# Two tokens per row for k and v, an attention output with fewer and wider matmuls, and a convolution by full diagonals, in a fused linear-attention and gated-unit kernel

## The chip, the cores and the metric

The kernel runs on one core of one Trainium2 chip. The metric is the device time of one execution in microseconds (us). Each kernel was run several times; medians are quoted with the number of runs. The medians are over all executions. Some of these were slow, which here means over 1.5% above the fastest of the same kernel in its job. The ratios use fast executions alone, and every profiled execution was a fast one. A profile's span is some 2 us shorter than the time of the same run (127.0 against 128.8 us for the kernel before).

Names of engines in the profile: PE is the matrix engine (PEld its weight loads), DVE the vector engine, ACT the scalar engine, POOL the general one, SP the one that issues the DMA transfers. PSUM is the memory that PE writes its results to. "Full clock" is a granted PE clock of 1.0 in the profile's records; before the first such record the matmuls ran at about half the pace. A "hole" is a stretch in which PE stands still without a wait that the profile shows.

## The reference

Four sequences of 768 tokens, eight heads of 48 channels. A recurrence keeps a 48x48 state per head; its output goes, heads side by side (384 channels), into a gated unit with a causal convolution of five taps.

```python
for t in range(S):
    cur = np.einsum('bhd,bhe->bhde', u[None] * kt, vt)          # bonus for the token itself
    y[:, :, t] = np.einsum('bhd,bhde->bhe', rt, state + cur)
    state = w[None, :, :, None] * state + np.einsum('bhd,bhe->bhde', kt, vt)
# x = y with the heads side by side
gate = sigmoid(sum over 5 taps of conv_w[tap] * shifted x)
val = x @ w_val
out = (gate * val) @ w_out
```

## The kernel before

Tokens are handled in chunks of 128. One pass of the main loop takes a unit of two chunks (cl = 0, 1) through one of four stages each: k transposes for unit i; bonus, scores, mask and state for unit i-1; attention output for unit i-2; convolution, value and projection for unit i-3. There are 12 units, so the loop has 15 passes.

```python
def load_kv(n, which):                       # 192 bytes per row and head
    ...
    d[n] = ld.tile([128, U, H, D], F32, name=f"{nm}_st")
    for cl in range(U):
        t0 = cu * W + cl * C
        nc.sync.dma_start(out=d[n][:, cl], in_=src[b, :, t0 : t0 + C, :].transpose([1, 0, 2]))

def y_out(n):                                # attention output: 32-column tiles
    for cl in range(U):
        y_ps = ps_mm.tile([128, NT, 128], F32, name="mm_ps")
        ...                                  # mm(G, ...): 32 columns, column group q = G % 4
        for G in range(3 * NP):              # state part
            mm(G, zf[:, 32 * G : 32 * G + 32], rT[:, G // 3, cl * C : cl * C + C])
        for x in range(2):                   # score part
            for h in range(H):
                ...
                mm(3 * p + (1 if x else 2 * par), vb[:, cl, 64*h+c0 : 64*h+c0+32], at[:, par, p, :])
        for G in range(3 * NP):              # bonus part
            mm(G, dv[:, cl, 32 * G : 32 * G + 32], ident, last=True)
        nc.scalar.copy(out=xT_t[b % 2][:, :, t0 : t0 + C], in_=y_ps)

def conv(n):                                 # 32x32 diagonals on 32x32 tiles
    for T0 in (0, 2):
        for t in range(KW):
            for q in range(4):
                for i in range(2):
                    ...
                    nc.tensor.matmul(out=g_ps[i][32*qo : 32*qo+32, o0 : o0+n0],
                                     lhsT=cwdiag[rows, T, t, :], rhs=xT[rows, T, ...], ...)
```

"Column group" below means one of the four strips of 32 columns of the PE array, set by the partitions that a matmul writes to; "row half" one of its two halves of 64 rows, set by the partitions that it reads. A "tile" of the array is a row part with a column part.

## Time and profile before

| | before |
|---|---|
| time, median of 4 runs | 128.5 us (128.04 to 129.91) |
| span of the profiled execution | 127.0 us |
| first convolution matmul | 34.2 us |
| PE matmuls | 2667 |
| chain that ended last | PE 58%, SPq 18%, issue 7%, DVE 6% |

The kernel has a first stage in which the loads fill the DMA engines, and a second stage from the first convolution on in which PE carries the chain. The chain is followed back from the last instruction, at each step to what released it. These are the three longest of the six waits of PE in the second stage of the kernel before (window 34 to 122 us): who waited for whom, then us in total, times, longest.

```profile
PE mm_ps L420 <- issue: 5.4, 3, 2.6
PE mm_ps L420 <- DVE cwdiag L206: 2.3, 1, 2.3
PE mm_ps L283 <- issue: 1.1, 2, 0.8
```

L420 is the convolution. "issue" means that PE stood still and the profile shows nothing that it waited for.

### The profile page before, as it was taken

What the parts mean: (1) busy time and instruction counts of PE and PEld (TensorE: products, weight loads), DVE (VectorE), ACT (ScalarE), POOL (GpSimd) and SP (SyncE); (2) the same over time, 40 slices, a digit from 0 to 9 for tenths busy, and PEclk for the clock granted to TensorE, in tenths of its full rate; (3) what the DMA queues carried; (4) which work ended last, traced back from release to release, by engine and by line L of the source; (5) the groups of instructions that cost most, each with busy time, mean ns of one, the idle gap of its engine ahead of it and who ended that gap; (6) DMA issues with size and microseconds to landing.
All of it is one profiled execution on the core that took longest, in us unless ns stands there. A gap on an engine that the chain in (4) does not pass through costs nothing.

```text
span 127.0 us, 5936 instructions
## 1 busy us (share of the span) xinstructions
PE 96.4 (76%) x2667; PEld 73.7 (58%) x2667; DVE 80.7 (64%) x134; ACT 64.6 (51%) x113; POOL 63.0 (50%) x90
## 2 busy tenths in 40 slices
PE   0036864865299749979994899999999999999950
PEld 0024643453188537767872666778777777777620
DVE  0559578733929619859695296596968978663030
ACT  4599800235452823745946506559492656264630
POOL 6925561485929807059796250597967050500000
PEclk9999999999999999999999859999999999999999
DMA  1999999999997979787599983973030030303203
GB/s 47 189 341 222 194 242 300 204 337 197 198 201 158 334 149 273 155 211 154 158 299 228 245 164 69 241 141 129 0 129 5 0 126 8 132 5 124 105 24 124
DMA packets 58675, 20.83 MB, mean 164 GB/s; under 512 B 50453, under 2 KB 58650, under 8 KB 58650
## 3 DMA queue, kind: packets, MB, share of 16 engines
q1 hardware_dynamic: 58522, 20.46, 66.0%
q8 instruction: 20, 0.33, 1.1%
q0 software_dynamic: 128, 0.00, 0.1%
q14 instruction: 5, 0.04, 0.1%
HBM read 15.74 MB, written 4.72 MB: 161 GB/s over the span
## 4 chain that ended last, share of the span: by engine, by line
PE 58%; SPq 18%; issue 7%; DVE 6%; DMA 4%; ACT 2%; DVEq 0%
PE mm_ps L420 11%; PE mm_ps L376 11%; SPq L72 10%; PE mm_ps L468 9%; PE mm_ps L439 6%; SPq L80 6%; PE at_ps L310 5%; DMA k_st<-in_k_dram 4%; PE tr_ps L263 4%; PE kv_ps L336 3%; PE mm_ps L448 3%; PE tr_ps L238 2%; PE mm_ps L283 2%; PE kv_ps L345 2%; ACT o_sb L475 2%
## 5 line engine op out<-in xcount | busy, mean ns | idle before, releaser
L296 POOL TENSOR_TENSOR dv<-v_st,s_sb 128x384 bf16<-128x384 f32 x24 | 19.4, 829 | 33.7 <-PE at_ps L310 31.5
L322 DVE TENSOR_TENSOR at<-at_ps,mask 128x1024 bf16<-128x1024 f32 x24 | 29.3, 1220 | 2.5 <-PE at_ps L310 1.6
L404 ACT CAST xT<-mm_ps 128x384 bf16<-128x384 f32 x24 | 11.5, 478 | 30.0 <-PE mm_ps L376 29.4
L255 POOL CAST vb<-v_st 128x384 bf16<-128x384 f32 x24 | 17.1, 733 | 9.1 <-DMA v_st<-in_v_dram 9.1
L420 PE MATMUL mm_ps<-xT,cwdiag 32*32 32x256 bf16 (+1 forms) x960 | 15.5, 253 | 7.7 <-issue 5.4
L226 POOL TENSOR_TENSOR rs<-r_st,dr 128x576 bf16<-128x576 f32 x13 | 18.6, 1448 | 3.8 <-DMA r_st<-in_r_dram 3.8
L420 PEld LDWEIGHTS <-cwdiag 32*32 32x32 bf16 x960 | 12.3, 93 | 11.6 <-issue 7.9
L429 ACT ACTIVATE gate<-mm_ps 128x384 bf16<-128x384 f32 x24 | 10.5, 494 | 13.3 <-PE mm_ps L420 13.3
L456 DVE TENSOR_TENSOR hT<-mm_ps,gate 128x384 bf16<-128x384 f32 x24 | 12.4, 549 | 6.5 <-PE mm_ps L448 6.3
L263 PE MATMUL tr_ps<-ident,ks 128*128 128x128 bf16 x96 | 9.1, 250 | 9.7 <-DVE ks L245 9.5
L245 DVE TENSOR_TENSOR ks<-k_st,dk 128x768 bf16<-128x768 f32 x12 | 12.9, 1079 | 4.7 <-DMA k_st<-in_k_dram 4.7
L266 ACT COPY kT<-tr_ps 128x1024 bf16<-128x1024 bf16 x12 | 12.3, 1024 | 6.5 <-PE tr_ps L263 6.4
L468 PE MATMUL mm_ps<-wout,hT 128*128 128x384 bf16 x72 | 14.0, 328 | 0.4 <-DVE hT L456 0.4
L239 ACT COPY rT<-tr_ps 128x768 bf16<-128x768 bf16 x16 | 12.3, 807 | 2.4 <-PE tr_ps L238 2.3
L292 DVE COPY s_sb<-mm_ps 128x16 f32<-128x16 f32 x12 | 2.1, 174 | 17.8 <-PE mm_ps L283 9.1
L263 PEld LDWEIGHTS <-ks 128*128 128x128 bf16 x96 | 6.7, 111 | 11.1 <-DVE ks L245 10.2
L475 ACT COPY o_sb<-mm_ps 128x384 f32<-128x384 f32 x24 | 11.5, 478 | 3.1 <-PE mm_ps L468 1.8
L439 PE MATMUL mm_ps<-xT,wval 128*128 128x256 bf16 x72 | 12.5, 284 | 0.0
L238 PE MATMUL tr_ps<-ident,rs 128*128 128x128 bf16 x96 | 9.3, 252 | 3.9 <-POOL rs L226 1.8
L310 PE MATMUL at_ps<-rT,kT 48*128 48x128 bf16 x192 | 10.8, 240 | 1.6 <-DVE at L322 1.5
L276 DVE TENSOR_TENSOR pr<-rT,kT 128x1024 bf16<-128x1024 bf16 x12 | 9.0, 748 | 3.8 <-ACT rT L239 3.8
L361 DVE TENSOR_TENSOR z<-kv_ps,wcm 128x384 bf16<-128x384 f32 x20 | 10.9, 547 | 0.0
(63 smaller groups left out, 140.9 us busy)
## 6 DMA issues: line engine op xcount, KB each, us to landing
k_st<-in_k_dram SPq DMA_DIRECT2D x24, 192.0 KB, 4.7
r_st<-in_r_dram SPq DMA_DIRECT2D x8, 576.0 KB, 6.3
v_st<-in_v_dram SPq DMA_DIRECT2D x24, 192.0 KB, 4.7
out_dram<-o_sb SPq DMA_DIRECT2D x12, 384.0 KB, 2.7
wv_st<-in_moe_w_val_dram SPq DMA_DIRECT2D x1, 576.0 KB, 5.0
wo_st<-in_moe_w_out_dram SPq DMA_DIRECT2D x1, 384.0 KB, 6.1
wo_st<-in_moe_w_out_dram SPq DMA_DIRECT2D x1, 288.0 KB, 6.6
w_bc<-in_w_dram SPq DMA_DIRECT2D x1, 192.0 KB, 3.7
```

What stands on the lines that cost most here:

```text
L226: eng.tensor_tensor(out=rs_t[p][:, :, :, 0:D].rearrange("p j a d -> p a j d"), in0=r_st[b][:, hs, :].rearrange("p a (j d) -> p a j d", d=D ...
L245: nc.vector.tensor_tensor(out=ks_t[n % 3][:, :, :, :, 0:D].rearrange("p c n a d -> p c (n a) d"), in0=k_st[n], in1=dk[:, None, :, :].to_br ...
L255: nc.gpsimd.tensor_copy(heads(vb[:, cl], H), v_st[n][:, cl])
L263: nc.tensor.transpose(tr[:, cl, p, :], ks[:, cl, p].rearrange("p a x -> p (a x)"), ident)
L296: nc.gpsimd.tensor_tensor(out=dv_t[n % 2][:, cl].rearrange("p (h d) -> p h d", d=D), in0=v_st[n][:, cl], in1=st["s", n][:, cl, :, None].to ...
L310: nc.tensor.matmul(out=at_ps[:, par, p, :], lhsT=kT[rows, p, cs], rhs=rT[rows, p, cs], start=(p == 0), stop=(p == NP - 1), skip_group_chec ...
L322: nc.vector.tensor_tensor(out=st["at", n, cl].rearrange("p a n i -> p (a n) i"), in0=st["at_ps", n, cl].rearrange("p a n i -> p (a n) i"), ...
L376: nc.tensor.matmul(out=y_ps[32 * q : 32 * q + 32, T, :], lhsT=lt, rhs=rh, start=q not in first, stop=last, skip_group_check=True,)
L420: nc.tensor.matmul(out=g_ps[i][32 * qo : 32 * qo + 32, o0 : o0 + n0], lhsT=cwdiag[rows, T, t, :], rhs=xT[rows, T, t0 + c0 + t : t0 + c0 + ...
L439: nc.tensor.matmul(out=v_ps[:, 0:W], lhsT=wval[:, kt, i, :], rhs=xT[:, kt, t0 : t0 + W], start=(kt == 0), stop=(kt == NT - 1), skip_group_ ...
L468: nc.tensor.matmul(out=o_ps, lhsT=hT[:, i, c0 : c0 + C], rhs=wout[:, 2 + cl if j == 2 else i, :], start=(j == 0), stop=(j == 2),)
L475: nc.scalar.copy(out=o_sb[:, cl, :], in_=o_ps)
```

## The change

The intent: load k and v in pieces of 384 bytes (two tokens of a head, which lie side by side) and so halve the packets; write the attention output with wider matmuls where that fits (64 columns, and 128 for the bonus), in the score and bonus parts with both chunks side by side on the two row halves; and make the convolution 15 matmuls with full 128x128 diagonals instead of 80 with 32x32 ones. A partition now holds tokens 2p and 2p+1 of the unit, so a chunk lies on 64 partitions, and the contractions over tokens split into j = 0, 1.

```diff
-            d[n] = ld.tile([128, U, H, D], F32, name=f"{nm}_st")
-            for cl in range(U):
-                t0 = cu * W + cl * C
-                nc.sync.dma_start(out=d[n][:, cl], in_=src[b, :, t0 : t0 + C, :].transpose([1, 0, 2]))
+            d[n] = ld.tile([128, H, 2, D], F32, name=f"{nm}_st")
+            nc.sync.dma_start(
+                out=d[n].rearrange("p h j d -> p h (j d)"),
+                in_=src[b, :, cu * W : cu * W + W, :].rearrange("h (p j) d -> p h (j d)", j=2))
 ... state: 8 matmuls of 64 rows instead of 4 of 128
-                lhsT=ks[:, cl, p].rearrange("p a x -> p (a x)"),
-                rhs=heads(vb[:, cl], H)[:, 2 * p : 2 * p + 2, :],
+            for j in range(2):
+                    lhsT=ks[rows, j, p].rearrange("p a x -> p (a x)"),
+                    rhs=vb[rows, j, 2 * p : 2 * p + 2, :],
 ... attention output: five phases, both chunks side by side
+        for m in (64, 32):                       # state part, 64 then 32 columns wide
+            for p in range(NP):
+                ... for cl in range(U): mm(cl, g, m, 0, C, z[...][:, g0 : g0 + m], rT[:, p, :, ...])
+        for m in (64, 32):                       # score part
+            for p in range(NP):
+                ... for par, g, c0 in parts: for j in range(2): for cl in range(U):
+                        mm(cl, g, m, 0, C, vb[rows, j, c0 : c0 + m], st["at", n, j][rows, par, p, :])
+        for j in range(2):                       # bonus part, 128 columns wide
+            for T in range(NT):
+                for cl in range(U):
+                    mm(cl, 4 * T, 128, 64 * j, 64, dv[rows, j, T * 128 : T * 128 + 128], ident[rows, rows])
 ... convolution
+                for t in range(KW):
+                    nc.tensor.matmul(out=g_ps[:, i, :], lhsT=cwdiag[:, T, t, :],
+                                     rhs=xT[:, T, t0 + t : t0 + t + W], start=(t == 0), stop=(t == KW - 1))
 ... cut: scores in 64x64 tiles, mask by token parity, value and projection in three plain blocks, preparation
```

## The prediction

> **What bounds the kernel now.** I read four views in this order: busy shares, slices, the chain that ended last in order of time, and the records of single matmuls and DMA packets.
>
> ```profile
> PE 96.4 (76%) x2667; PEld 73.7 (58%) x2667; DVE 80.7 (64%) x134; ACT 64.6 (51%) x113; POOL 63.0 (50%) x90
> PE   0036864865299749979994899999999999999950
> DMA  1999999999997979787599983973030030303203
> PE 58%; SPq 18%; issue 7%; DVE 6%; DMA 4%; ACT 2%; DVEq 0%
> 24.85 5.48 DMA k_st<-in_k_dram
> 30.42 0.96 DVE ks L245
> ```
>
> The slices show two stages. Up to about 31 us the DMA engines are full and PE has holes; the chain there is SP issuing loads against full queues, then the load of the fourth k tile (lands at 30.33 us). From 34 us (first convolution) to 122 us the chain is PE nearly throughout. One undisturbed pass of that second stage:
>
> ```profile
> 84.45 1.08 PE mm_ps L468 x6
> 85.54 0.67 PE tr_ps L238 x12
> 86.21 1.02 PE mm_ps L420 x78
> 87.23 0.55 PE tr_ps L263 x8
> 87.78 0.18 PE mm_ps L283 x8
> 87.96 0.33 PE at_ps L310 x8
> 88.29 0.28 PE kv_ps L336 x4
> ...
> 90.05 1.23 PE mm_ps L376 x80
> ```
>
> The third column is the time on the chain: projection 1.08, r transposes 0.67, convolution 1.02 (1.16 in other passes), k transposes 0.55, bonus 0.18, scores 0.33, state 0.28, attention output 1.23. No wait for another engine stands in it. DVE has 6.64 us of work per pass (0.96 ks, 0.69 pr, 0.17 s, 2 x 1.22 mask, 2 x 0.55 z, 2 x 0.52 hT, and what sharing adds), so it is close behind PE's 6.8, but behind.
>
> Two holes of PE matter, both inside the convolution:
>
> ```profile
> 43.69 2.64 issue
> 68.19 2.27 issue
> ```
>
> PE waits there for nothing that the profile shows. Beside each stands an instruction-fetch packet of 16 KB (256 instructions) on the DMA queue kind "instruction", starting at 43.8 and 67.6 us. I read the holes as PE outrunning its instruction supply: 160 PE instructions in 1.16 us. After the second, the matmuls run at half rate from 72.4 to 75.8 us, a further 1.7 us.
>
> **What the records say about PE.** Within the attention output (L376, 128x32 tiles) matmuls start in fours 3 to 5 ns apart, and fours are 56 ns apart: four column groups run at once, and two matmuls on the same column group follow each other at 56 ns, the streaming of 128 columns. Scores (48-row tiles) go in pairs, 56 ns between pairs. State matmuls on the full array (96 columns) are 42 to 43 ns apart, value (256 columns) 109 ns. Where the shape of the tile changes, the next start comes 146 to 154 ns after the last one instead of 56 (convolution to transposes 154, scores to state 148, scores to output 146, output to projection 152): about 0.09 us lost per change, 8 changes per pass.
>
> **What the Trainium skill says.** "TensorEngine Tiling (Array Packing)", Key Properties: changing the tiling mode drains TensorE, changing the tile alone does not. The trace agrees (146 to 154 against 56 ns). "TensorE: Matmul & The Clock Gate", Part 3, says matmuls start and end strictly in program order while distinct tiles overlap; the fours agree. So a matmul whose tile is busy holds up those behind it. "DMA: Bandwidth & Descriptors", Specifications, puts the size for line rate at 512 B or more. The trace: packets of 192, 1152 and 1536 B take a median of 15, 51 and 66 ns, thus near 8 ns plus 0.038 ns per byte.
>
> **The change, part by part.**
>
> *Loads.* k and v packets go from 192 to 384 B and halve in number (49152 to 24576). By the line through those three points a 384 B packet takes about 22.5 ns, estimate. A k or v tile is then 64 packets per engine, 1.44 us, instead of 128 x 15 = 1.92; with the mean-to-median excess about 0.5 us saved per tile, 12 us of DMA time in all, 3.6 us before the fourth k tile (seven tiles precede or are it), plus 0.6 us for the output weights, which are no longer loaded with a duplicate. That tile would land at about 26 instead of 30.3 us. But PE then takes over as the bound there: the old passes 0 to 2 end at 27.5 us at the half clock and depend on compute chains, one more Exp on ACT (0.6 us) delays them, the first attention output grows by about 1.8 us at that clock, and twelve r transposes (1.3) and the diagonals follow. I get a first convolution at about 32.5 instead of 34.2 us. Building the full diagonals costs DVE 3 x 640 elements, some 0.8 us each by the size of the 768-element ks op at 0.96; the old four copies and three products took 2.7 us, so it is even.
>
> *Convolution.* 80 matmuls on 32x32 tiles (1.16 us with its drain) become 15 on the full array with 256 columns: 15 x 109 = 1.64 us. The change back to the full array before the transposes goes (0.55 to 0.45). Net +0.38 us per pass, 12 passes: +4.6.
>
> *State.* Each chunk's contraction of 128 is split in two of 64 in the same row half: 8 matmuls at 43 ns instead of 4, and identity times z is now a change of shape: 0.28 to 0.43 and 0.16 to 0.25. From the first convolution on there are 16 state calls and 13 identities: 16 x 0.15 + 13 x 0.09 = +3.6.
>
> *Scores.* 16 matmuls of 64x64 tiles, four at once, 56 ns per four: 4 x 56, as before. About even, +0.02 for more weight loads.
>
> *Attention output, the decisive part.* 80 become 76, but I count rounds by tile, in program order:
> - z, 64 wide: two pairs use the lower column half, then two the upper, both chunks on the same columns: 8 matmuls one after another but for one overlap, ends at 395 ns.
> - z, 32 wide: columns 2,2,3,3,0,0,1,1: each pair serial, 289 ns.
> - values, 64 wide, 64 rows: the two chunks run at once; j and the pairs are serial within a column half: 8 rounds, one overlapped, 394 ns.
> - values, 32 wide: 8 groups of two serial rounds, each overlapping the next: about 525 ns.
> - bonus values, 128 wide and 64 columns: six pairs at 27 to 55 ns, about 245.
> Sum 1.85 us, and six drains of 0.09 (entry and five changes of shape) = 2.39 us against 1.23. Fewer instructions, yet fewer of them at once. +1.16 us in each of the 11 calls after the first, less 0.3 in the three first chunks of a batch without z: +11.9.
>
> *Projection.* Both chunks now finish together, so the second projection needs the buffer of the first xT copy, which starts later: +0.15 us, 12 times, +1.8. Value, bonus, mask, hT and the copies keep their element counts; POOL's halves merge and save about 0.3 us per pass off the path.
>
> *What shrinks.* PE instructions per pass fall from some 400 in 6.8 us to 290 in 9, so most of the fetch holes and the half-clock stretch (together some 8 us) should go: I credit 5. The PE waits for DVE and ACT in the second stage (roughly 5 us, such as 0.79 us for the mask at 47.84 and 2.4 us for rT at 91.9) lie beside longer PE work: credit 3.
>
> Sum: +4.6 + 3.6 + 0.4 + 11.9 + 1.8 - 5 - 3 - 1.7 = +12.6 us, giving 141. The largest items rest on six drains per output call and on serial same-column matmuls; I have no measurement of the new shapes, and errors there would mostly make it better, so I take 139.
>
> **Rivals.**
> 1. *The loads are the bound and halving the packets wins.* For it: DMA above 90% until about 73 us, and the chain starts with 24 us of SP issue. It would give 122 to 126. Against it: after 34 us PE has no wait on ks or r data from DMA in the list of waits (the 9.5 us for ks are two waits before 31 us), and PE work fills the time saved.
> 2. *Fewer instructions win: issue limits PE.* For it: 7% "issue" on the chain, and 2091 matmuls instead of 2667. If all of these holes went and the output stayed near 1.3 us, the sum would be about 130 to 132. Against it: the undisturbed pass runs in rounds of 56 ns set by columns, not by instruction count.
> 3. *Drains happen only between some shapes* (full array against rows, say), or the 64-wide phases overlap better than in my count. An output call at 1.8 us and no drain at the identity would take 6.5 + 1.2 us off: about 133.
> 4. *DVE becomes the bound.* At 6.64 us per pass against 9 for PE it can't, unless the permuted reads of k and dk double the 0.96 us of ks, which still leaves it below.
> 5. *Worse than counted.* 64-wide weight loads or two row halves not running at once would give 145 and more.
>
> **Range and chances.** The middle is 139; rival 3 and some of 2 set the low end at 130, rival 5 the high end at 146. Faster by over 2% needs rival 1 and a cheap output together, 0.06. Within 2% (126.2 to 131.4) needs rival 3 with nearly all credits, 0.11. Slower 0.83.
>
> **What would show it.** Right: the output line of the changed kernel takes 2.0 to 2.6 us per call on the chain, the convolution 1.6, two transposes-to-scores passes some 8.5 to 9 us apart; DVE share falls below 62%; DMA 384 B packets at 21 to 25 ns; first convolution at 31 to 34 us; hardly any "issue" on the chain inside the convolution. Wrong: an output call near 1.3 us (tiles overlap across program order, or shapes change without drain), passes of 7 us, or a first convolution at 28 us, which would mean the prologue hung on loads alone.

## The result, and the profile after

The changed kernel takes 133.34 us (median of 4 runs, 132.54 to 134.18) against 128.5 us. Ratios here are the mean time of one kernel's fast runs over that of the other's of the same rounds, so they are not quite the ratio of the medians. This one is 1.0358, with a 95% interval of 1.0248 to 1.0469. A later reading of the same pair gave 1.0518 (1.0409 to 1.0628). The first one may be too small: in its job the kernel before took 128.04 to 129.91 us, in the later ones 125.96 to 128.19 when fast. The direction was forecast, and so was the cause in part, but the forecast was +8.2% (139 over 128.5), and the measured slowdown, 3.6 to 5.2%, is about half of that.

The page of the changed kernel: span, busy time by engine, busy tenths of PE and DMA in 40 slices, and the engines' shares of the chain.

```profile
span 130.8 us, 4712 instructions
...
PE 109.4 (84%) x2091; PEld 81.7 (62%) x2091; DVE 82.4 (63%) x131; ACT 63.2 (48%) x114; POOL 57.7 (44%) x67
...
PE   0033874996999999999999999999999999998950
...
DMA  3899999989990942827998339020300303003113
...
PE 71%; DVE 13%; ACT 7%; DMA 3%; issue 2%; DVEq 0%
```

From slice 11 on PE is busy without a break, where before it had dips to 4 and 7. "issue" has fallen from 7% to 2%, and SP has left the chain. PE executes fewer matmuls and is busy for longer. A clean pass on its chain (start, us, what):

```profile
97.95 1.60 PE mm_ps L379 x76
99.56 1.21 PE mm_ps L483 x6
100.77 1.64 PE mm_ps L443 x15
102.41 0.45 PE tr_ps L267 x8
...
103.38 0.44 PE kv_ps L341 x8
103.82 0.27 PE kv_ps L350
```

Attention output (L379) 1.60 us instead of 1.23, projection 1.21 instead of 1.08, convolution 1.64 instead of 1.16, k transposes 0.45 instead of 0.55, state 0.44 instead of 0.28. All of these but the first are the predicted numbers. The first was predicted as 2.39. The waits of PE in its second stage (33 to 126 us):

```profile
PE mm_ps L443 <- DVE cwdiag L215: 1.1, 1, 1.1
PE mm_ps L379 <- DVE hT L471: 1.1, 5, 0.3
PE mm_ps L483 <- DVE hT L471: 0.5, 1, 0.5
```

The issue waits are gone altogether. The second line is a new wait. Five times the output call begins with one matmul and stands still before the others. The timeline of the changed kernel around one of these shows it (start, us, group, and in brackets the idle time before the group with what ended it):

```profile
62.94 0.42 PE L313 MATMUL at_ps<-rT,kT 48*64 48x128 bf16 x16
63.28 0.24 PE L379 MATMUL mm_ps<-rT,z 128*64 128x128 bf16 x1
63.70 0.66 PE L379 MATMUL mm_ps<-rT,z 128*64 128x128 bf16 x15 [0.18 <-DVE hT L471]
```

By the code, the two chunks are now written in turn into two PSUM tiles, and with three buffers in the ring the second tile is the buffer that the first value tile has just left; DVE reads that one (hT) after its mask and its decay. It happens where no second state update comes before the output. Four such calls take 2.02 us instead of 1.61, and the fifth, which is the last call, 2.20. No run tested this with another buffer; it is read from the trace and the code.

To see where the time went I summed, from the records of single matmuls, the time from each matmul's start to the next one's, by stage, from the first convolution on:

| stage | before, us | after, us | change |
|---|---|---|---|
| convolution and k transposes | 25.0 | 24.4 | -0.6 |
| bonus, scores, value, r transposes | 31.0 | 26.6 | -4.4 |
| state and identity | 6.0 | 9.9 | +3.9 |
| attention output | 13.7 | 19.4 | +5.7 |
| projection | 12.6 | 13.1 | +0.5 |
| sum | 88.3 | 93.4 | +5.1 |
| first convolution starts at | 34.2 | 32.8 | -1.4 |

Together +3.7 us, the difference of the two spans (130.8 and 127.0) but for rounding. The first line hides two things that cancel: the convolution's own work grew as forecast, and its holes went. The second line is the other holes, and the half-clock stretch of the kernel before (72.4 to 75.8 us), which the changed kernel has nowhere between 31.3 and 130.3 us. In both lines there is also a difference of the clock that isn't work: the kernel before came to full clock only at 38.3 us, 4.1 us after its first convolution began, and the changed kernel 1.4 us before it.

### The profile page after: what moved, and what is told of

The parts are those of the page before. It is cut to its first block, busy times and chain, and to the rows that moved or that the text cites. A ratio compares the mean times of both kernels' runs of the same rounds, so it can differ in the third digit from the quotient of the medians.

```text
span 130.8 us, 4712 instructions
## 1 busy us (share of the span) xinstructions
PE 109.4 (84%) x2091; PEld 81.7 (62%) x2091; DVE 82.4 (63%) x131; ACT 63.2 (48%) x114; POOL 57.7 (44%) x67
## 4 chain that ended last, share of the span: by engine, by line
PE 71%; DVE 13%; ACT 7%; DMA 3%; issue 2%; DVEq 0%
PE mm_ps L443 15%; PE mm_ps L379 15%; PE mm_ps L483 11%; DVE at L325 7%; PE at_ps L313 6%; PE mm_ps L463 6%; PE tr_ps L239 5%; PE kv_ps L341 5%; PE tr_ps L267 4%; DMA w_bc<-in_w_dram 3%; DVE hT L471 3%; ACT dr L137 2%; PE kv_ps L350 2%; PE mm_ps L285 2%; ACT rT L240 1%
## 5 line engine op out<-in xcount | busy, mean ns | idle before, releaser
L297 POOL TENSOR_TENSOR dv<-v_st,s_sb 128x768 bf16<-128x768 f32 x12 | 17.7, 1475 | 46.7 <-DVE s_sb L294 46.6
L443 PE MATMUL mm_ps<-xT,cwdiag 128*128 128x256 bf16 x180 | 22.0, 272 | 1.2 <-DVE cwdiag L215 1.1
L443 PEld LDWEIGHTS <-cwdiag 128*128 128x128 bf16 x180 | 17.0, 97 | 4.5 <-DVE cwdiag L215 1.8
L471 DVE TENSOR_TENSOR hT<-mm_ps,gate 128x512 bf16<-128x512 f32 (+1 forms) x24 | 12.2, 549 | 8.9 <-PE mm_ps L463 8.9
L246 DVE TENSOR_TENSOR ks<-k_st,dk 128x768 bf16<-128x768 f32 x12 | 14.9, 1245 | 0.7 <-ACT dk L132 0.6
L259 POOL CAST vb<-v_st 128x768 bf16<-128x768 f32 x12 | 12.9, 1076 | 5.3 <-DMA v_st<-in_v_dram 5.2
L450 ACT ACTIVATE gate<-mm_ps 128x512 bf16<-128x512 f32 (+1 forms) x24 | 11.2, 495 | 4.6 <-PE mm_ps L443 4.5
L313 PE MATMUL at_ps<-rT,kT 48*64 48x128 bf16 x384 | 10.9, 236 | 0.8 <-DVE at L325 0.6
L341 PE MATMUL kv_ps<-vb,ks 64*128 64x96 bf16 x160 | 11.5, 218 | 0.0
L463 PEld LDWEIGHTS <-wval 128*128 128x128 bf16 x108 | 10.3, 97 | 1.8
```

Source lines behind the costliest of these rows:

```text
L246: nc.vector.tensor_tensor(out=ks_t[n % 3][:, :, :, :, 0:D].rearrange("p j n a d -> p j (n a) d"), in0=k_st[n].rearrange("p h j d -> p j h d"),
L297: nc.gpsimd.tensor_tensor(out=dv_t[n % 2].rearrange("p j (h d) -> p j h d", d=D), in0=v_st[n].rearrange("p h j d -> p j h d"), in1=st["s", ...
L313: nc.tensor.matmul(out=at_ps[cs, par, p, :], lhsT=kT[rows, p, j, cs], rhs=rT[rows, p, :, cs], start=(p == 0), stop=(p == NP - 1), skip_gro ...
L341: nc.tensor.matmul(out=kv_ps[:, p], lhsT=ks[rows, j, p].rearrange("p a x -> p (a x)"), rhs=vb[rows, j, 2 * p : 2 * p + 2, :], start=(p == ...
L443: nc.tensor.matmul(out=g_ps[:, i, :], lhsT=cwdiag[:, T, t, :], rhs=xT[:, T, t0 + t : t0 + t + W], start=(t == 0), stop=(t == KW - 1),)
L463: nc.tensor.matmul(out=v_ps[:, i, :], lhsT=wval[:, kt, T * 128 : T * 128 + 128], rhs=xT[:, kt, t0 : t0 + W], start=(kt == 0), stop=(kt == ...
```

## The experiments

Theory A: a later matmul whose tile of the array is free starts past earlier ones that wait for a busy tile. Rival B, the assumption of my count: matmuls start strictly in program order. Rival C: two matmuls on the same columns run at once if they write different PSUM banks. For the holes: they come from PE using up instructions faster than they arrive (density), or from instruction fetch standing behind the loads (traffic). The runs in one table, each against the kernel before of its own job. The medians of the kernel before include slow executions, so go by the ratio; in the row of e8 the two even point in different directions.

| run | median, us | before, us | ratio (95%) | full output call, us |
|---|---|---|---|---|
| e1, tile order | 135.38 | 128.19 | 1.0675 (1.054 to 1.081) | 1.78 |
| e2, taken in turn | 132.33 | 128.19 | 1.0362 (1.024 to 1.049) | 1.55 |
| e3, before, blocks of ten | 140.29 | 128.19 | 1.1001 (1.090 to 1.110) | 3.13 |
| e4, output 32 wide | 139.81 | 128.19 | 1.0973 (1.087 to 1.107) | 1.51, up to 2.86 with holes |
| e5, before with full diagonals | 123.61 | 127.63 | 0.9720 (0.966 to 0.978) | 1.23 |
| e6, after with small diagonals | 135.12 | 127.63 | 1.0609 (1.050 to 1.072) | 1.61 |
| e7, after with 192-byte loads | 134.68 | 127.63 | 1.0569 (1.049 to 1.064) | 1.61 |
| e8, before, blocks of five | 127.99 | 128.79 | 1.0108 (1.002 to 1.019) | 1.47 |
| e9, after again | 133.80 | 128.79 | 1.0518 (1.041 to 1.063) | 1.61 |

All outputs are right.

**e1_tilemajor and e2_roundrobin: the order inside the phases.** Both collect the matmuls of a phase and emit them in another order.

```diff
-        def mm(cl, G, m, c0, cn, lt, rh):
+        def mm(*a):
+            todo.append(a)
...
+        flush(lambda a: (a[1] % 4, a[0]))      # e1: column group, then chunk
+        flush()                                # e2: first matmul of every tile, then the second, ...
```

> The changed kernel, with the matmuls of each phase of the output call put in order of their tile (column group, then chunk), so that up to four or six of the same tile follow each other. Theory A (a later matmul on a free tile starts past earlier ones that wait for a busy tile, over at least this many instructions): the order doesn't matter, a full output call stays at 1.60 us on the chain, ratio to the changed kernel within 0.5%, so some 133 us and 1.035 to 1.04 against before. Rival B (matmuls start strictly in program order, as I predicted): by counting rounds a call takes about 3.7 us, 11 calls cost over 20 us more, above 150 us. Rival C (two matmuls on the same columns run at once where they write different PSUM banks): the 64-wide z phase goes from 4 to 8 rounds, +0.2 us a call, about 135 to 136 us. A look-ahead that is too short for this would lie between A and B.

> The changed kernel, with the matmuls of each phase taken in turn from every tile, the best order for strict program order. Theory A: no change, output call 1.60 us, 133 us. Rival B: a call falls well below 1.60 us (rounds 4+2+4+4+6 as a floor are already 1.5 us with drains, so at most 0.1 us to gain), 132 us. The value of this run is as the pair of the one in tile order: A says equal, B says 20 us apart.

B falls: a call in tile order takes 1.78 us, not 3.7. C falls too: the 64-wide z phase lasts 0.354 us in tile order and 0.355 in the changed kernel, although in tile order the two chunks no longer alternate. A holds with a limit, which I had not put into its number. In the two z phases a tile's matmuls stand together equally long in both orders, so it is the score and bonus phases that test A. By phase (from its first matmul to the next phase's first), tile order against the changed kernel: z 64 wide 0.354 and 0.355, z 32 wide 0.236 and 0.235, scores 64 wide 0.377 and 0.367, scores 32 wide 0.457 and 0.369, bonus 0.353 and 0.281. Where six of one tile follow each other, or four of one tile with many tiles behind, something is lost, and elsewhere nothing. The whole output stage sums to 21.2 us in e1, 19.4 in the changed kernel and 18.5 in e2. The rest of e1's difference is in part the clock: PE ran at full clock from 36.0 us on in e1's execution and from 31.5 in e2's, which is visible in the convolution sum (21.1 and 20.1 us).

**e3_before_groupmajor: the same in the kernel before, with blocks of ten.**

```diff
+            for a in sorted(todo, key=lambda a: a[0] % 4):   # ten on one column group, then the next ten
+                mm_now(*a)
```

> The kernel before, with the 40 matmuls of each chunk's output sorted by column group: ten on one group, then ten on the next. Theory A with a long look-ahead (40 matmuls with their weight loads): 1.23 us per call as before, time within 1% of before. Rival B: ten rounds of 56 ns per group with hardly an overlap, 2.24 us per chunk, 4.5 us per call instead of 1.23; 12 calls give +35 us or more, about 165 us. A look-ahead of about 8 to 16 matmuls would give something between, say 1.6 to 3.5 us per call.

This run shows the reordering itself. In the built program the order for a column group is three rT,z, then four at,vb, then three ident,dv, then the next group's three rT,z. The timeline of this run, PE, groups in order of start:

```profile
93.94 0.34 PE L381 MATMUL mm_ps<-rT,z 128*32 128x128 bf16 x3
94.12 0.39 PE L381 MATMUL mm_ps<-at,vb 128*32 128x128 bf16 x4
94.29 0.23 PE L381 MATMUL mm_ps<-rT,z 128*32 128x128 bf16 x1
94.34 0.22 PE L381 MATMUL mm_ps<-ident,dv 128*32 128x128 bf16 x1
94.36 0.22 PE L381 MATMUL mm_ps<-rT,z 128*32 128x128 bf16 x1
94.40 0.22 PE L381 MATMUL mm_ps<-ident,dv 128*32 128x128 bf16 x1
94.41 0.22 PE L381 MATMUL mm_ps<-rT,z 128*32 128x128 bf16 x1
94.45 0.22 PE L381 MATMUL mm_ps<-ident,dv 128*32 128x128 bf16 x1
```

The fourth rT,z starts at 94.29 us, before the first of the three ident,dv that stand ahead of it in the program, and they then alternate. It passes three waiting matmuls, and it did not start earlier, when four or more waited. A call takes 3.13 us: less than the 4.5 that I counted for strict order, far more than the 1.23 of the original order. So A is right and its reach is short.

**e8_before_blocks5: how far the reach goes.** As e3, in blocks of five.

```diff
-            for a in sorted(todo, key=lambda a: a[0] % 4):
+                keyed.append((seen[q] // 5, q, a))            # blocks of five per column group
```

> The kernel before with the 40 matmuls of each chunk's output in blocks of five on one column group (the run with blocks of ten took 3.13 us per call against 1.23 in the order of before). In that run a matmul of the next group started first when only three matmuls of the old group were still waiting. If three is how many waiting matmuls a later one can pass (A with a short look-ahead), blocks of five lose about half a block each: 1.6 to 2.0 us per call, 133 to 138 us. If the look-ahead counts something longer (eight matmuls or more), 1.23 to 1.35 us and about 128 us. Strict order (B) would give 5 rounds per block without overlap, about 3.7 to 4.5 us per call, over 150 us.

A call takes 1.47 us, below the 1.6 that a reach of exactly three gave in my count and above the 1.35 of a long one. The order shows again that later matmuls start first, and strict order is out of the question. How many waiting matmuls can be passed, and whether row halves count apart, isn't settled; "a few" fits e1, e3 and e8. The time rose by 1.1% (0.2 to 1.9), some 1.4 us, although 11 calls at +0.23 us are +2.5 us: the issue waits of the convolution fell from 5.4 to 4.1 us in this execution, and those of the bonus from 1.1 to 0.3.

**e4_after_32wide: narrow matmuls, fewer changes of tile shape.**

```diff
-        for m in (64, 32): ...                 # five phases, 76 matmuls
+        for G in range(3 * NP): ...            # z, 32 columns on 128 rows: 24
+        for x in range(2): ...                 # scores, 32 columns on 64 rows: 64
+        for j in range(2): ...                 # bonus, 32 columns on 64 rows: 48
```

(The expected text says 160 matmuls; the code has 136.)

> The changed kernel, with the output call all in 32-column tiles again (z on 128x32, values and bonus values on 64x32): 160 matmuls instead of 76, one inner change of tile shape instead of four. If the drain of 93 ns per change of shape and rounds per tile set the time (A): rounds 6 x 56 + 8 x 56 + 6 x 28 = 0.95 us and two or three drains, 1.15 to 1.25 us per call instead of 1.60, 11 calls give -4 us: about 129 us. If the number of instructions sets it (rival: fewer, wider is better): 160 matmuls take longer than 76, and instruction-fetch holes come back as issue waits of 0.5 to 2.6 us; 133 us or more.

The gain that I expected from drains did not come. Without holes the three phases of one call take 0.46, 0.55 and 0.50 us, 1.51 together: the narrow bonus phase takes 0.50 instead of 0.28 us, since its 48 matmuls start some 8 ns apart, which is slower than six rounds (a round is one matmul on every tile in use at once). That is 0.10 us less than the 1.61 of the wide call, not the 0.35 to 0.45 that I expected. And the holes are back, now inside the output (the first three of five lines):

```profile
PE mm_ps L379 <- issue: 3.7, 5, 1.1
PE mm_ps L379 <- DVE hT L462: 1.1, 5, 0.4
PE mm_ps L434 <- issue: 0.7, 1, 0.7
```

So within this layout the wide matmuls are right, and my preference for narrow ones was wrong. What they buy is fewer instructions and no holes. Not all of the +6.5 us over the changed kernel is this: e4's execution came to full clock at 36.0 us, the changed kernel's at 31.3.

**e5_before_fullconv: the convolution part alone.** The kernel before, with convolution, value, projection and weight preparation of the changed kernel.

```diff
-                            lhsT=cwdiag[rows, T, t, :],       # 32x32 tiles, 80 per unit
+                        lhsT=cwdiag[:, T, t, :],              # full array, 15 per unit
```

> The kernel before with the convolution, value and projection of the changed kernel (full diagonals, 15 matmuls of 256 columns instead of 80 on 32x32 tiles; 30 PE instructions instead of 160 per convolution), loads and attention as before. My count: the convolution costs 12 x 0.38 = 4.6 us more on PE. If the holes of 2.6, 2.3, 0.8 and 0.5 us in the convolution come from PE outrunning its instruction supply, they go, and with them the stretch at half clock: -6 to -8 us, net 124 to 127 us, ratio 0.97 to 0.99. If the holes came from DMA traffic (instruction fetch behind the loads, which are here as before), they stay, and the time is 133 us, ratio 1.035.

It is faster than both kernels: 123.61 us, 0.972. Its waits of PE in the second stage (window 34 to 118 us), complete:

```profile
PE mm_ps L441 <- DVE hT L429: 0.5, 1, 0.5
PE mm_ps L401 <- DVE cwdiag L200: 0.4, 1, 0.4
```

No issue wait is left, with the old loads and all of their packets. The convolution stage sums to 21.9 us against 20.1 with the holes; bonus and value, which fell by 1.3 and 1.1 us, pay for part. The first convolution starts at 32.7 instead of 34.2 us. Of these 1.5 us, 0.8 are the fourth k tile, which landed at 29.5 instead of 30.3 us in this execution; the rest is preparation, where four small copies for the diagonals (1.7 us of DVE) are gone and the first product takes longer. Full clock came at 38.0 us, as in the kernel before (38.3), so the gain is not an earlier clock; the half-clock stretch of 72.4 to 75.8 us is gone with the holes, as expected.

**e6_after_tileconv: the other way round.** The changed kernel with the small diagonals.

> The changed kernel with the convolution, value and projection of before (80 matmuls on 32x32 tiles). PE gets 12 x 0.38 = 4.6 us shorter. If density of instructions makes the holes: holes of 0.5 to 2.6 us are back in the convolution although the loads have half the packets, time 131 to 136 us. If DMA traffic makes them: no holes, 128.5 to 129.5 us.

Holes are back, in the scores, the convolution and the output. Lines of its chain in order of time:

```profile
65.71 0.86 issue
...
70.86 0.81 issue
...
76.26 1.33 issue
```

The convolution stage falls by 4.2 us (15.9 instead of 20.1), as counted, and more than that is lost elsewhere: from the first convolution to the last matmul it takes 96.2 us against 93.8. The holes are 3.2 us of that loss. The clock may be more: full clock came only at 42.7 us, 9.6 us after the first convolution began, and at half the pace that costs up to 4.8 us (an estimate). So e6's time proves nothing, but its holes do: its loads have the same half number of packets as the changed kernel's. Small diagonals bring holes with half the packets, and e5 has none with all of them (DMA share 0.88 from 34 to 84 us, in the kernel before 0.86). Density is needed.

What I had missed, and what the records of single instructions settle, is where the holes lie. I number PE's instructions (weight loads and matmuls) from 0 in order of start. In the second stages of the kernel before, e3, e4, e6 and e8 there are 23 issue waits of over 0.15 us, and every one of them ends at an instruction whose number is 189 more than a multiple of 256. One instruction packet (16,384 bytes; 20 in the kernel before, 16 in the changed one, 0.9 to 1.7 us each in the former) comes per 256 PE instructions, nearly. Each wait ends 2.3 to 3.1 us after the start of the last such packet before it. So a hole is the wait for the next block of 256 instructions.

Traffic has a part too, which no run isolates. In the kernel before, the packets ahead of the two long holes started 3.7 and 3.5 us after PE had begun the block before, while loads ran; from 84 us on (DMA share 0.22) it was at most 2.1 us, and no hole there reaches 0.3 us with convolutions as dense. But loads aren't needed for a hole: e4 has one of 1.09 us at 105 us, where the DMA share is 0.12.

**e7_after_192 and e9_after_again: what the loads are worth.**

```diff
-            nc.sync.dma_start(out=... "p h (j d)", in_=... "h (p j) d -> p h (j d)")
+            for j in range(2):
+                nc.sync.dma_start(out=d[n][:, :, j], in_=rows[:, :, j])     # 192 bytes again
```

> The changed kernel with k and v loaded as 192-byte pieces again into the same layout (two transfers per tile, one per token parity). My prediction says the loads are worth only 1 to 2 us, because PE and not the loads sets the start of the first convolution: first convolution at 33 to 34.5 us instead of 32.8, time 133.5 to 135 us, ratio to before 1.035 to 1.05. Rival: the loads are worth their 8.6 us of DMA time or the 3.6 us at the fourth k tile: 137 us or more.

> The changed kernel itself once more, five rounds, as a second reading of the ratio to before (1.0358 with four runs): 1.03 to 1.05, with output calls of 1.42, 1.61 and 2.03 us as in the first trace. It tells how far the start of full clock (31.3 us in the first trace) varies between executions, and so how much of the difference to the run with 192-byte loads (full clock from 38.7 us) is the loads.

The medians are 134.68 and 133.80 us. The interval of e7's ratio overlaps with that of e9 and lies just above that of the first reading (up to 1.0469). The mean of e7's six executions is 134.35 us, that of the nine fast ones of the changed kernel from its two jobs 133.32. So the loads are worth about 1 us, though e7's k and v packets took 55.9 us of DMA time and e9's 40.2. The profiled executions differ by 2.2 us in span (133.0 and 130.7). In e7 the loads are back on the chain:

```profile
PE 66%; SPq 17%; DVE 6%; DMA 5%; issue 2%; ACT 1%; DVEq 0%
```

The first convolution starts at 33.2 instead of 32.5 us, and full clock comes at 38.7 instead of 30.9 us. In the two executions of the changed kernel it came at 31.3 and 30.9. Whether the later clock in e7 follows from the loads or from chance isn't shown. The other traces lean to the loads: in the five profiled executions with 192-byte loads (before, e3, e5, e7, e8) lasting full clock came between 38.0 and 38.8 us, in the six with 384-byte loads at 30.9, 31.3, 31.5, 36.0, 36.0 and 42.7. The rival, that the loads are worth 3.6 us or more, falls.

## Why the prediction was wrong

**The first convolution** (predicted 32.5 us): 32.8. Right, and for the reason given: the chain there is no longer SP and loads but ACT, DVE and PE.

**384-byte packets** (about 22.5 ns): median 22 ns. But their mean is 26.35, so the DMA time of k and v fell from 49152 x 15.98 / 16 = 49.1 us to 24576 x 26.35 / 16 = 40.5 us: 8.6 us saved, not 12. In the sum only the first stage rests on it.

**Convolution** (1.64 us, transposes 0.45): measured so. **State and identity** (+3.6 us): +3.9. **Scores** (even): 0.35 against 0.33 us a call. **Projection** (+1.8): from first start to the next stage's, the call grew by 0.13 us where r transposes follow, as counted, but by only 0.04 where the convolution follows, since with full diagonals the change of shape between the two is gone. In the kernel before, the last call was 0.33 us longer than in the changed one, so the sum grew by 0.5.

**Attention output** (2.39 us a call, +11.9 us): this step failed. The sentence was "a matmul whose tile is busy holds up those behind it". It doesn't: e3 shows later matmuls starting first.

The trace of the kernel before, on which the prediction was built, already spoke against it. The fours that it took as agreeing with program order do not. By the code, the last eight of a chunk's 16 score matmuls stand in the program on column groups 1, 1, 0, 0, 3, 3, 2, 2. In strict order they would need five rounds after the two of the first eight. The bonus part would start together with the last of these seven, so six rounds of 56 ns, 0.34 us, after the score part. It starts four rounds after it, 0.22 us (0.23 in the timeline, which rounds):

```profile
90.15 0.40 PE L376 MATMUL mm_ps<-at,vb 128*32 128x128 bf16 x16
90.38 0.34 PE L376 MATMUL mm_ps<-ident,dv 128*32 128x128 bf16 x12
```

What counts is therefore the longest queue of any single tile, not the rounds in program order. Counted so, the phases have 4, 2, 4, 4 and 6 rounds (56 ns each, 27 in the last), and with a drain per phase (the 0.09 us that a change of tile shape costs) that gives about 0.32, 0.20, 0.32, 0.32 and 0.26, 1.41 us together; they measured 0.355, 0.235, 0.367, 0.369 and 0.281, 1.61 us in all. So this count is still 0.2 us short. The six drains of my sum were there: from the last matmul of a phase to the first of the next it is 146 to 150 ns within the call, about 160 once in each of the calls where one chunk has no z part, and 122 after the bonus phase, whose matmuls are half as long. Of rival 3, the first half (some changes of shape cost nothing) is refuted; its other half (the 64-wide phases overlap better than in my count) is what happened. Its figure of about 133 us is also what was measured, but by other terms: it counted no drain at the identity, where there is one. The stage as a whole grew by 5.7 us, of which about 2.2 are the new wait for hT (four calls at 0.41 us more than 1.61, and the last at 0.59), which I had not foreseen.

**The holes and DVE waits** (credit 5 + 3 us): convolution and transposes were to grow by 4.6 and fell by 0.6, so about 5 us of holes went there; bonus, value, r transposes and scores fell by 4.4 more, where I expected +0.4. About 10 us against a credit of 8, a little more than said; the reading of the holes, PE using up its instructions faster than they come, was right. That the total came out near is in part luck: some 2 us of it (half of the 4.1 us at half pace after the first convolution, an estimate) are the earlier full clock, which I had not counted. Rival 2 (fewer instructions win) is thus right in its mechanism, and e5 shows what it is worth when nothing else is changed; in the changed kernel the growth of state and output outweighs it.

In the sum: +12.6 predicted, +3.8 in the span measured. The output term is 6.2 us too large. The holes and waits gave 2.0 more than credited, and the projection cost 1.3 less; state (+0.3) and the first stage (-1.4 instead of -1.7) went the other way. That makes up the 8.8 us between the two, but for rounding.

## What to carry to other kernels

Count a phase of small matmuls by the longest queue on one tile of the array, plus a drain for each change of tile shape, not by strict program order; but keep runs on one tile short, because only a few waiting matmuls are passed. A prediction's rule of order can be tested on the trace at hand before it is used: compare the order of starts with the program. Look for stretches where PE uses up its instructions fast (160 in 1.16 us here), above all while loads run: fewer and wider matmuls there can pay even where each step takes longer, as the full diagonals did with the value and projection that go with them (0.972). When a change bundles parts, run each part by itself; here one part was a gain, one about nothing, and one a loss.

## What the Trainium skill lacked or had wrong

- "TensorE: Matmul & The Clock Gate", Part 3: it says matmuls are a strict FIFO in start and end, without reordering. In e3 a matmul started at 94.29 us ahead of three that precede it in the program (94.34, 94.40 and 94.45 us); blocks of ten on one column group took 3.13 us a call where my count for strict order gives 4.5, and blocks of five 1.47.
- "TensorEngine Tiling (Array Packing)", Key Properties: it has the drain but no figure. Here it is about 0.09 us (146 to 154 ns between starts instead of 56), also where only the column width changes (128x64 to 128x32: 150 ns).
- "Runtime: NRT & Kernel Launch", Instruction fetch mechanics: it says that instructions come in blocks of 16 KiB (256 of them) by DMA, which the packets of 16,384 bytes here agree with, and calls the cost of crossing a block mostly hidden. With 80 matmuls and 80 weight loads in 1.16 us the kernel before stood still for up to 2.6 us, 6.7 us in all in its second stage, each time at the start of a new block of 256; e5, with 30 such instructions per convolution, not at all.
